# A fused attention and MLP kernel on one core: x^T in two PSUM tensors, four products ahead of the numerators, key features behind the numerators, last results by halves

## The chip, the core and the metric

The kernel runs on one core of a Trainium2 chip. A core has five engines with instruction streams of their own: PE (matrix products out of SBUF into PSUM), DVE and ACT (elementwise work; both read PSUM), POOL (elementwise work on SBUF) and SP (which here only starts DMA transfers). They meet through semaphores. The metric is the device time of one execution in microseconds; several executions are given as a median.

## The reference

Four batches of four heads, 1088 tokens, head dimension 32. Queries and keys are turned into 64 features each, and attention is linear in them; the result then goes through an MLP with an exact GELU.

```python
def phi(x):
    a = np.einsum('rd,bhsd->bhsr', S1, x)          # 8 values
    b = np.einsum('rd,bhsd->bhsr', S2, x)          # 8 values
    return np.einsum('bhsi,bhsj->bhsij', a, b).reshape(*x.shape[:-1], 64)
q_p, k_p = phi(q), phi(k)
kv  = np.einsum('bhsf,bhsd->bhfd', k_p, v)
z   = np.sum(k_p, axis=2)
num = np.einsum('bhsf,bhfd->bhsd', q_p, kv)
den = np.einsum('bhsf,bhf->bhs', q_p, z)[..., None] + 1e-06
x   = (num / den)                                   # then (B,H,S,D) -> (B*S, H*D) = (4352, 128)
h   = x @ w_in                                      # 128 -> 2048
g   = 0.5 * h * (1.0 + erf(h / sqrt(2)))
out = g @ w_out                                     # 2048 -> 128
```

## The kernel before

**Tiling.** Tokens are worked on in nine chunks. Chunks 0 to 7 have 512 tokens each, two for each batch; chunk 8 holds the 64 tokens left over from each of the four batches, 256 in all. For a chunk the kernel makes the query features (`expand_products`, `expand_copy`, `expand_multiply`), divides numerators by denominators (`attend_by_token` for chunks 0 and 1, `attend` for the others) into the transposed attention result x^T, and runs the MLP: 16 hidden products (`hidden`, L551), each 128 hidden channels wide, with a GELU on ACT (L558), and the products with w_out. Chunks 0 and 1 use plain projections (`project`, L667); chunks 2 to 7 replace these by Strassen-like products of half size (`two_products`, L624), whose sums of activations POOL forms (L593 to L596) and whose results `drain` and `combine` put together.

**Weights.** They arrive as 64-bit numbers. `Rounding` turns them into float32 in steps: `fields` (two DVE operations, L252 and L254, into `bits_e` and `bits_a`), `exponents` (ACT, L260, `bits_r`), `low_words` (ACT, L248, `bits_low`), `mantissas` (L268 on DVE, or L265 on ACT and L266 on POOL, `bits_m`), `signs` (DVE, L273, into `bits_e`), `product` (L278). The first two pieces of w_in and of w_out hold 256 columns, four hidden tiles in all: the first w_out piece serves the projections of tiles 0 and 1, the second those of tiles 2 and 3. Later pieces hold 512 columns.

**Keys.** For each batch `key_turn_blocks` turns the keys (DVE), `key_features` makes the two sets of eight values by 64 small PE products (L348, two calls of 32), copies one factor out with ACT (`a_t`, L361) and multiplies the outer product on DVE (`k_p`, L362). `add_tokens` adds token pairs, `kv_sum` forms kv on PE (L391), and `turn_kv` (L429) transposes it, through ACT copies `kv_T` and `kz`. `attend(n)` takes the numerators and denominators with four PE products (L494), copies the denominators out with ACT (`den`, L500, four copies), inverts them on DVE (L502), and multiplies (L506) into x^T.

**PSUM.** Eight banks: `h_ps` has two tensors of one bank (hidden products), `o_ps` two of one bank (projections), `w_ps` two of two banks (everything of attention). A reading engine is made to wait for another engine that reads the same PSUM tensor.

**Order.** It is written out by hand. A header runs the attention of batch 0 in straight lines. Behind it the steps are (chunk, hidden tile): chunks 0 and 1 alternate in groups of four tiles, then come chunks 2 to 8 of 16 tiles each. `at(t, f)` puts attention work into step t, `products`, `done` and `drains` do so for the other parts. In a step come the hidden product, then the slots, then stores, then products that fall due, two steps or more behind their GELU. The last lines of the function make every engine follow the order of the text.

The lines of the header and of the first steps that matter here:

```python
    attend_by_token(0, banks)
    ...
    w_in[1].product(pool)
    w_out[0].fields()
    turn_x(0, hidden_bank())
    ...
        if t == 3:
            attend_by_token(1, halves(work_banks()), lambda: (w_out[1].mantissas(), ...))
        if t == 4:
            turn_x(1, work_bank())
            for f, *a in products[t]:
                f(*a)
```

`turn_x` transposes the attention result of chunks 0 and 1 with four PE transposes into one PSUM tensor (L304); ACT copies its first half (L533), DVE its second (L534).

`store(8)`, at the end, copies the last chunk's two halves out of one PSUM tensor, the first with DVE and the second with ACT (L673), and starts two DMAs on SP and two on ACT's queue (L675).

Of the kernel before, what the change touches and what calls it, by code (L numbers as in the profile page):

```python
# [8 lines left out]
FP = mybir.dt.float32  # L9
# [7 lines left out]
def kernel(  # L17
# [20 lines left out]
    R = S1.shape[0]  # L38
# [196 lines left out]
    class Rounding:  # L235


        def __init__(self, dst):
            self.dst, self.wide = dst, dst.name in raw
            if self.wide:  # L240
                rows, n = dst.shape
                self.lo, self.hi = raw[dst.name][:, :, 0], raw[dst.name][:, :, 1]
                self.a, self.e, self.r = (mlp.tile([128, LC], U32, name=f"bits_{x}")[:rows, :n] for x in "aer")
                self.low, self.m = (mlp.tile([128, LC], FP, name=f"bits_{x}")[:rows, :n] for x in ("low", "m"))
# [55 lines left out]
    def transposed(ps, name, srcs, copy):  # L300

        n = len(srcs) * 128
        for i, s in enumerate(srcs):
            pe.transpose(ps[:, i * 128:(i + 1) * 128], in_=s, identity=ident)  # L304
        t = att.tile([128, CW], FP, name=name, bufs=3 if name == "xT" else 2)
        copy(out=t[:, :n], in_=ps[:, :n])
        return t
# [33 lines left out]

    def key_features(b, r, banks, by_pool=()):

        for i in range(2 * NCH):
            for c in range(2):
                for t in range(2):
                    at = i * 128 + c * 64
                    pe.matmul(banks[t][c * 64:(c + 1) * 64, i * 32:(i + 1) * 32],  # L348
                              lhsT=kT[r][t * 64:(t + 1) * 64, at:at + 64],
                              rhs=S12[t * 64:(t + 1) * 64, 2 * t:2 * t + 2].rearrange("p h r -> p (h r)"),  # L350
                              start=True, stop=True)

        k_p[b, r] = att.tile([128, 2, J, R, R], FP, name="k_p")
# [74 lines left out]
    def turn_kv(b, ps, copy):  # L428
        pe.transpose(ps[:, :128], in_=kv_T[b], identity=ident)  # L429
        copy(out=kz[b].rearrange("p c n -> p (c n)"), in_=ps[:, :128])  # L430
# [55 lines left out]
    def attend(n, meanwhile=lambda: None):  # L486

        W = width[n]
        owners = [(0, W, n // NCH)] if n < NMAIN else [(i * REM, (i + 1) * REM, i % 2 * 2 + i // 2) for i in range(B)]
        banks = halves(work_banks())  # L490
        for (c0, c1, b) in owners:
            for c in range(NP):
                for r in range(2):
                    pe.matmul(banks[r][c * F:(c + 1) * F, c0:c1], lhsT=kz[b][r * F:(r + 1) * F, c, :],  # L494
                              rhs=qp[n][r * F:(r + 1) * F, c, c0:c1], start=True, stop=True)
        den = att.tile([128, CW], FP, name="den")
        for h in range(H):
            c, r = h // 2, h % 2
            at = c * F + (1 - r) * D
            act.activation(out=den[h * D:(h + 1) * D, :W], in_=banks[r][at:at + D, :W], func=ACT.Copy, bias=1e-6)  # L500
        meanwhile()
        dve.reciprocal(out=den[:, :W], in_=den[:, :W])  # L502
# [27 lines left out]

    def turn_x(n, ps):
        def by_both(out, in_):
            by_act(out=out[:, :CW // 2], in_=in_[:, :CW // 2])  # L533
            by_dve(out=out[:, CW // 2:], in_=in_[:, CW // 2:])  # L534

        xT[n] = transposed(ps, "xT", [x_tok[n][:, j].rearrange("p h d -> p (h d)") for j in range(JC)], by_both)

# [47 lines left out]
    def token_sums(n, b):  # L585
# [4 lines left out]
        for j, (name, dtype) in enumerate((("bits_a", U32), ("bits_e", U32), ("bits_low", FP), ("bits_m", FP))):  # L590
            t = mlp.tile([128, LC], dtype, name=name)
            s[j + 1] = (t if dtype == FP else t.bitcast(FP)).rearrange("p (e x) -> p e x", e=2)
# [62 lines left out]

    def project(n, fi):
        first, final = fi == 0, fi == NF - 1
        if first:
            o_of[n] = out_bank() if n < NMAIN else work_bank()
        g = g_of.pop((n, fi))  # L660
        if n == NMAIN:

            for i in range(B // 2):
                pe.matmul(o_of[n][:, i * 128:(i + 1) * 128], lhsT=g[:, i * 128:(i + 1) * 128], rhs=w_tile(w_out_sb, fi),  # L664
                          start=(first and i == 0), stop=final, skip_group_check=True)
            return
        pe.matmul(o_of[n], lhsT=w_tile(w_out_sb, fi), rhs=g, start=first, stop=final)  # L667

    def store(n):
        oT = mlp.tile([128, JC, d_model], FP, name="oT")  # L670
        if n == NMAIN:
            for i, (copy, eng) in enumerate(((by_dve, sp), (by_act, act))):
                copy(out=oT[:, i, :], in_=o_of[n][:, i * 128:(i + 1) * 128])  # L673
                for b in (i, i + 2):
                    eng.dma_start(out=out[b * S + MAIN:(b + 1) * S, :], in_=oT[b // 2 * REM:(b // 2 + 1) * REM, i, :])  # L675
            return
# [75 lines left out]
    w_out = [Rounding(w) for w in w_out_sb[:2]]  # L752
    w_out[0].low_words()
# [4 lines left out]
    w_in[1].product(pool)  # L758
    w_out[0].fields()
    turn_x(0, hidden_bank())  # L760
    keep_busy(1, bank)
    w_out[0].exponents()
    expand_copy(1, 2)
    expand_multiply(1, 0)
    w_out[0].finish()
    w_out[1].low_words()

# [9 lines left out]
    def features(b, r):  # L777
        key_features(b, r, halves(work_banks()))

    held = {}  # L780
# [18 lines left out]

    at(0, expand_copy, 1, 3)  # L800
    at(0, expand_multiply, 1, 1)
    at(1, lambda: (w_out[1].fields(), w_out[1].exponents()))
    for i, (t0, t1) in enumerate(((4, 6), (8, 10), (12, 20))):
# [18 lines left out]
    for n in range(3, NCHUNK):  # L822
# [20 lines left out]
    for t, (n, fi) in enumerate(steps):  # L843
# [4 lines left out]
        elif n == NMAIN:  # L848
            at_ = max(t + LAG, (n * NF + 5) if fi < 3 else (n * NF + 6) if fi < 5 else 0)
            products[at_].append((project, n, fi))  # L850
            if fi == NF - 1:
                done[at_ + 1].append(n)
        elif fi % NB == NB - 1:
# [73 lines left out]
```

## Time and profile before

| what | value |
|---|---|
| three runs, median | 278.21 us (277.94 to 278.29) |
| the profiled execution | 278.03 us |
| its span in the profile | 276.2 us |
| PE instructions | 2209 |
| PE's granted clock over the span | 0.998 |
| DMA | 13.49 MB, 49 GB/s in the mean |

| stretch of the span, us | what runs | PE busy | DVE | ACT | POOL |
|---|---|---|---|---|---|
| 0 to 18.29 | loads, attention of batch 0 up to chunk 0's first hidden product | 15.93 | 14.39 | 11.84 | 7.12 |
| 18.29 to 26.63 | up to chunk 1's first hidden product | 8.28 | 6.88 | 4.25 | 1.28 |
| 26.63 to 66.00 | chunks 0 and 1, attention of batch 1 | 39.37 | 24.60 | 22.02 | 12.16 |
| 66.00 to 260.00 | chunks 1 to 7 | 194.00 | 100.65 | 99.48 | 124.22 |
| 260.00 to 272.10 | chunk 8 | 12.05 | 4.26 | 5.06 | 0.00 |
| 272.10 to 276.20 | last copies and stores | 0.00 | 0.28 | 0.27 | 0.00 |

A row of the profile's timeline gives the start in us, the duration, the engine, the line of the source, the operation, what it writes and reads, and shapes; in brackets the engine's idle time before it and who ended that. PEld is PE's weight load. A float32 product shows as two records, a float32 transpose as one, and small products that run side by side in parts of the array overlap; the tile shape of the array (128\*128, 128\*64, 64\*64, 32\*128) stands after the operands. Ends of PE records are modelled, so starts are the better measure.

### The profile page before, as it was taken

What the parts mean: (1) busy time and instruction counts of PE and PEld (TensorE: products, weight loads), DVE (VectorE), ACT (ScalarE), POOL (GpSimd) and SP (SyncE); (2) the same over time, 40 slices, a digit from 0 to 9 for tenths busy, and PEclk for the clock granted to TensorE, in tenths of its full rate; (3) what the DMA queues carried; (4) which work ended last, traced back from release to release, by engine and by line L of the source; (5) the groups of instructions that cost most, each with busy time, mean ns of one, the idle gap of its engine ahead of it and who ended that gap; (6) DMA issues with size and microseconds to landing.
All of it is one profiled execution on the core that took longest, in us unless ns stands there. A gap on an engine that the chain in (4) does not pass through costs nothing.

```text
span 276.2 us, 5543 instructions
## 1 busy us (share of the span) xinstructions
PE 269.6 (98%) x2209; PEld 134.9 (49%) x2209; DVE 151.1 (55%) x248; ACT 142.9 (52%) x282; POOL 144.8 (52%) x158
## 2 busy tenths in 40 slices
PE   8989999999999999999999999999999999999993
PEld 6744444543432455445444555444444454455793
DVE  6987688424953565079308965479037902750230
ACT  4683764356454634484348433674358344733441
POOL 3331000952003896457875877368766886777300
PEclk9999999999999999999999999999999999999999
DMA  6659263636201200000200001000200020011020
GB/s 210 188 155 325 47 167 62 160 76 161 42 0 29 34 16 2 2 0 1 40 0 1 2 2 34 7 0 2 38 0 2 0 40 0 1 24 18 4 38 19
DMA packets 37914, 13.49 MB, mean 49 GB/s; under 512 B 28288, under 2 KB 37248, under 8 KB 37888
## 3 DMA queue, kind: packets, MB, share of 16 engines
q1 hardware_dynamic: 37648, 13.05, 18.8%
q8 instruction: 17, 0.28, 0.5%
q10 hardware_dynamic: 240, 0.08, 0.1%
q14 instruction: 9, 0.07, 0.1%
HBM read 10.90 MB, written 2.23 MB: 48 GB/s over the span
## 4 chain that ended last, share of the span: by engine, by line
PE 96%; DVE 2%; ACT 0%; issue 0%
PE h_ps L551 43%; PE o_ps L624 27%; PE o_ps L667 10%; PE w_ps L453 3%; PE w_ps L664 3%; PE w_ps L494 2%; PE w_ps L391 1%; PE w_ps L696 1%; PE w_ps L348 1%; PE o_ps L400 1%; PE h_ps L304 1%; PE h_ps L520 0%; PE w_ps L420 0%; PE w_ps L520 0%; PE o_ps L304 0%
## 5 line engine op out<-in xcount | busy, mean ns | idle before, releaser
L551 PE MATMUL h_ps<-xT,w_in 128*64 128x512 f32 (+3 forms) x490 | 141.0, 577 | 1.1 <-DVE xT L534 1.0
L558 ACT ACTIVATE block<-h_ps 128x512 f32<-128x512 f32 (+1 forms) x112 | 63.4, 566 | 84.6 <-PE h_ps L551 83.7
L551 PEld LDWEIGHTS h_ps<-xT,w_in 128*64 128x64 f32 (+1 forms) x490 | 43.2, 146 | 38.0 <-issue 14.4
L593 POOL TENSOR_TENSOR bits_low<-block 128x512 f32<-128x512 f32 x24 | 30.8, 1284 | 52.8 <-ACT block L558 52.6
L624 PE MATMUL o_ps<-block,w_out 128*64 128x256 f32 x192 | 49.5, 380 | 0.0
L474 DVE TENSOR_TENSOR q_pT<-A_sb,w_ps 64x512 f32<-64x512 f32 x32 | 22.1, 691 | 43.0 <-ACT A_sb L460 42.3
L624 PEld LDWEIGHTS o_ps<-block,w_out 128*64 128x64 f32 x192 | 25.7, 137 | 32.4 <-issue 24.5
L594 POOL TENSOR_TENSOR bits_a<-block 128x512 f32<-128x512 f32 x24 | 30.6, 1274 | 12.9 <-ACT block L558 12.8
L667 PE MATMUL o_ps<-g,w_out 128*128 128x512 f32 x64 | 33.5, 604 | 0.0
L596 POOL TENSOR_TENSOR bits_m<-block,bits_e 128x512 f32<-128x512 f32 x24 | 30.6, 1276 | 1.9
L595 POOL TENSOR_TENSOR bits_e<-bits_a,block 128x512 f32<-128x512 f32 x24 | 30.6, 1274 | 1.9
L558 ACT ACTIVATE g<-h_ps 128x512 f32<-128x512 f32 x32 | 19.1, 596 | 21.2 <-PE h_ps L551 21.1
L502 DVE RECIPROCAL den<-den 128x512 f32<-128x512 f32 (+1 forms) x7 | 21.8, 3115 | 10.7 <-ACT den L500 10.7
L624 PE MATMUL o_ps<-bits_a,small 128*64 128x256 f32 x96 | 24.9, 382 | 0.0
L624 PE MATMUL o_ps<-bits_low,small 128*64 128x256 f32 x96 | 24.7, 380 | 0.0
L624 PE MATMUL o_ps<-block,small 128*64 128x256 f32 x96 | 24.7, 380 | 0.0
L624 PE MATMUL o_ps<-bits_m,w_out 128*64 128x256 f32 x96 | 24.6, 379 | 0.0
L624 PEld LDWEIGHTS o_ps<-block,small 128*64 128x64 f32 x96 | 13.0, 137 | 15.8 <-issue 11.7
L460 ACT COPY A_sb<-w_ps 64x512 f32<-64x512 f32 (+1 forms) x36 | 17.7, 557 | 3.1 <-PE w_ps L453 2.9
L506 DVE TENSOR_TENSOR xT<-w_ps,den 32x512 f32<-32x512 f32 (+1 forms) x28 | 18.2, 649 | 1.0
L667 PEld LDWEIGHTS o_ps<-g,w_out 128*128 128x128 f32 x64 | 11.3, 190 | 14.5 <-issue 13.6
L500 ACT ACTIVATE den<-w_ps 32x512 f32<-32x512 f32 (+1 forms) x28 | 15.6, 557 | 2.0 <-PE w_ps L494 1.7
(158 smaller groups left out, 295.9 us busy)
## 6 DMA issues: line engine op xcount, KB each, us to landing
block<-in_moe_w_in_dram SPq DMA_DIRECT2D x3, 512.0 KB, 7.9
block<-in_moe_w_out_dram SPq DMA_DIRECT2D x3, 512.0 KB, 10.6
k<-in_k_dram SPq DMA_DIRECT2D x48, 32.0 KB, 1.8
v<-in_v_dram SPq DMA_DIRECT2D x3, 512.0 KB, 4.3
q<-in_q_dram SPq DMA_DIRECT2D x24, 64.0 KB, 3.8
out_dram<-oT SPq DMA_DIRECT2D x24, 64.0 KB, 2.2
k<-in_k_dram SPq DMA_DIRECT2D x2, 256.0 KB, 3.1
q<-in_q_dram SPq DMA_DIRECT2D x2, 256.0 KB, 4.2
```

The costliest lines, as they stand in the source:

```text
L460: act.copy(out=A[g // 2][F:, g % 2, :width[n]], in_=B_of[n][g // 2][:F, g % 2, :width[n]])
L474: dve.tensor_mul(out=cols[r * F:(r + 1) * F], in0=a[:, :, r::2], in1=b[:, :, r::2])
L502: dve.reciprocal(out=den[:, :W], in_=den[:, :W])
L506: dve.tensor_mul(out=xT[n][rows, :W], in0=banks[h % 2][rows, :W], in1=den[rows, :W])
L551: pe.matmul(ps[rows, :W], lhsT=w[:, rows], rhs=xT[n][:, :W], start=True, stop=True)
L558: act.activation(out=g_of[n, fi][:, :W], in_=ps[:, :W], func=ACT.Gelu)
L593: pool.tensor_sub(out=s[3], in0=a11, in1=a21)
L594: pool.tensor_add(out=s[1], in0=a21, in1=a22)
L595: pool.tensor_sub(out=s[2], in0=s[1], in1=a11)
L596: pool.tensor_sub(out=s[4], in0=a12, in1=s[2])
L624: pe.matmul(acc[n][bank][half * 64:(half + 1) * 64, col:col + HW], lhsT=fixed, rhs=moving, start=b == 0 and e == 0 and name in "4715", sto ...
L667: pe.matmul(o_of[n], lhsT=w_tile(w_out_sb, fi), rhs=g, start=first, stop=final)
```

## The change

- **x^T of chunks 0 and 1.** `turn_x` takes two PSUM tensors, two transposes into each; ACT copies the first, DVE the second. `fields` of w_out's first piece moves ahead of the token attention of chunk 0.
- **Chunk 0's four hidden products first.** Steps 0 to 3 run only `hidden(0, t)`; then come chunk 1's numerators (`attend_by_token(1)`), then the projections of tiles 0 and 1, then chunk 1's transposes, the projection of tile 2 and chunk 1's first hidden product. The query features of chunk 1 are finished before step 0. The first w_out piece is finished on DVE in step 0; the second piece's mantissas move to ACT and POOL, its product from POOL to DVE.
- **Key features of batches 2 and 3.** They move from eleven steps behind the start of the chunk to five, into `attend`, right after the numerators; the 64 products share one PSUM tensor, the four `a_t` copies stand ahead of the `den` copies, and `k_p` and the token sums follow x^T. The key turns move from inside `attend` to seven steps ahead of it. Batch 1 stays as it was.
- **kv of batches 2 and 3** is turned by two 64-column float32 products with the identity in place of one transpose.
- **The last chunk** has a PSUM tensor for each half; the last two tiles' projections run half by half; three of the four last stores are on SP, one on ACT.
- `bits_a` and `bits_e` have three buffers each, `kT_rem` one of 128 columns.

```diff
-    def turn_x(n, ps):
-        def by_both(out, in_):
-            by_act(out=out[:, :CW // 2], in_=in_[:, :CW // 2])
-            by_dve(out=out[:, CW // 2:], in_=in_[:, CW // 2:])
-
-        xT[n] = transposed(ps, "xT", [x_tok[n][:, j].rearrange("p h d -> p (h d)") for j in range(JC)], by_both)
+    def turn_x(n, banks):
+
+        xT[n] = att.tile([128, CW], FP, name="xT", bufs=3)
+        for i, ps in enumerate(banks):
+            for j in range(2):
+                pe.transpose(ps[:, j * 128:(j + 1) * 128], in_=x_tok[n][:, 2 * i + j].rearrange("p h d -> p (h d)"),
+                             identity=ident)
+        for i, (ps, copy) in enumerate(zip(banks, (by_act, by_dve))):
+            copy(out=xT[n][:, i * 256:(i + 1) * 256], in_=ps[:, :256])
...
     def turn_kv(b, ps, copy):
-        pe.transpose(ps[:, :128], in_=kv_T[b], identity=ident)
+        if b < 2:
+            pe.transpose(ps[:, :128], in_=kv_T[b], identity=ident)
+        else:
+            for rows in (slice(0, 64), slice(64, 128)):
+                pe.matmul(ps[rows, :128], lhsT=kv_T[b][:, rows], rhs=ident, start=True, stop=True)
...
+        meanwhile()
         den = att.tile([128, CW], FP, name="den")
         for h in range(H):
...
-        meanwhile()
         dve.reciprocal(out=den[:, :W], in_=den[:, :W])
...
+    w_out = [Rounding(w) for w in w_out_sb[:2]]
+    w_out[0].fields()
     attend_by_token(0, banks)
...
-    turn_x(0, hidden_bank())
+    turn_x(0, [hidden_bank(), hidden_bank()])
...
+    def features_of_all(b):
+        banks = halves(work_banks())
+        for r in range(2):
+            key_products(r, banks, r * 128)
+        held["keys"] = banks
+        held["factors"] = []
+        for r in range(2):
+            a = att.tile([128, 2, J, 2 * R], FP, name="a_t")
+            for t in range(2):
+                act.copy(out=a[:, t, :, 0:R], in_=factors(banks[t], r)[:, :, 0:R])
+            held["factors"].append(a)
...
+    def outer_of_all(b):
+        for r, a in enumerate(held["factors"]):
+            k_p[b, r] = att.tile([128, 2, J, R, R], FP, name="k_p")
+            for t in range(2):
+                dve.tensor_mul(**spread(k_p[b, r][:, t], a[:, t, :, 0:R], factors(held["keys"][t], r)[:, :, R:2 * R]))
+        for r in range(2):
+            add_tokens(b, r, dve)
...
-        at(t + 5, attend, n, lambda b=b, keys=keys: [key_turn_blocks(b, r) for r in range(2) if keys])
         if keys:
+            for r in range(2):
+                at(t - 2, key_turn_blocks, b, r)
+        at(t + 5, attend, n, lambda b=b, keys=keys: keys and features_of_all(b))
+        if keys:
+            at(t + 5, outer_of_all, b)
             at(t + 8, widen_v_rem, b)
-            for r in range(2):
-                at(t + 11, features, b, r)
-            for r in range(2):
-                at(t + 11, add_tokens, b, r, dve)
...
+            if fi < NF - 2:
+                products[at_].append((project, n, fi))
             if fi == NF - 1:
+                products[at_] += [(project, n, f, (i,)) for i in range(B // 2) for f in (fi - 1, fi)]
                 done[at_ + 1].append(n)
...
     for t in range(len(steps) + LAG):
-        if t == 3:
-            attend_by_token(1, halves(work_banks()), lambda: (w_out[1].mantissas(), w_out[1].signs(),
-                                                              w_out[1].product(pool)))
+        if t < 4:
+            hidden(0, t)
+            if t == 0:
+                w_out[0].exponents()
+                w_out[0].finish()
+                w_out[1].fields()
+            if t == 3:
+                attend_by_token(1, halves(work_banks()), lambda: (w_out[1].exponents(), w_out[1].low_words(),
+                                                                  w_out[1].mantissas(by_pool=True)))
+                w_out[1].signs()
+                w_out[1].product()
+                for u in range(4):
+                    for f, *a in products[u]:
+                        f(*a)
+            continue
         if t == 4:
-            turn_x(1, work_bank())
+            turn_x(1, [work_bank(), work_bank()])
```

More of the change, by code (lines that the diff above doesn't have):

```diff
@@ L242, in __init__ @@
                 self.lo, self.hi = raw[dst.name][:, :, 0], raw[dst.name][:, :, 1]
-                self.a, self.e, self.r = (mlp.tile([128, LC], U32, name=f"bits_{x}")[:rows, :n] for x in "aer")
+                self.a, self.e, self.r = (mlp.tile([128, LC], U32, name=f"bits_{x}", bufs=2 if x == "r" else 3)[:rows, :n]
+                                          for x in "aer")
                 self.low, self.m = (mlp.tile([128, LC], FP, name=f"bits_{x}")[:rows, :n] for x in ("low", "m"))
@@ L304, in transposed @@
             pe.transpose(ps[:, i * 128:(i + 1) * 128], in_=s, identity=ident)
-        t = att.tile([128, CW], FP, name=name, bufs=3 if name == "xT" else 2)
-        copy(out=t[:, :n], in_=ps[:, :n])
+        t = att.tile([128, n], FP, name=name, bufs=1 if name == "kT_rem" else 2)
+        copy(out=t, in_=ps[:, :n])
         return t
@@ L340, in spread, with key_products @@
                     in1=b[:, :, None, :].broadcast_to([128, n, R, R]))
-    def key_features(b, r, banks, by_pool=()):
+    def key_products(r, banks, col=0):
         for i in range(2 * NCH):
@@ L347, in key_features @@
                     at = i * 128 + c * 64
-                    pe.matmul(banks[t][c * 64:(c + 1) * 64, i * 32:(i + 1) * 32],
+                    pe.matmul(banks[t][c * 64:(c + 1) * 64, col + i * 32:col + (i + 1) * 32],
                               lhsT=kT[r][t * 64:(t + 1) * 64, at:at + 64],
@@ L351, in key_features @@
                               start=True, stop=True)
+    def key_features(b, r, banks, by_pool=()):
+        key_products(r, banks)
         k_p[b, r] = att.tile([128, 2, J, R, R], FP, name="k_p")
@@ L590, in token_sums @@
         for j, (name, dtype) in enumerate((("bits_a", U32), ("bits_e", U32), ("bits_low", FP), ("bits_m", FP))):
-            t = mlp.tile([128, LC], dtype, name=name)
+            t = mlp.tile([128, LC], dtype, name=name, bufs=3 if dtype == U32 else 2)
             s[j + 1] = (t if dtype == FP else t.bitcast(FP)).rearrange("p (e x) -> p e x", e=2)
@@ L654, in combine, with project @@
         return N[:, 1]
-    def project(n, fi):
+    def project(n, fi, parts=range(B // 2)):
         first, final = fi == 0, fi == NF - 1
         if first:
-            o_of[n] = out_bank() if n < NMAIN else work_bank()
-        g = g_of.pop((n, fi))
+            o_of[n] = out_bank() if n < NMAIN else [work_bank() for i in range(B // 2)]
+        g = g_of[n, fi]
         if n == NMAIN:
-            for i in range(B // 2):
-                pe.matmul(o_of[n][:, i * 128:(i + 1) * 128], lhsT=g[:, i * 128:(i + 1) * 128], rhs=w_tile(w_out_sb, fi),
-                          start=(first and i == 0), stop=final, skip_group_check=True)
+            for i in parts:
+                pe.matmul(o_of[n][i][:, :128], lhsT=g[:, i * 128:(i + 1) * 128], rhs=w_tile(w_out_sb, fi),
+                          start=first, stop=final)
             return
@@ L672, in store @@
             for i, (copy, eng) in enumerate(((by_dve, sp), (by_act, act))):
-                copy(out=oT[:, i, :], in_=o_of[n][:, i * 128:(i + 1) * 128])
-                for b in (i, i + 2):
-                    eng.dma_start(out=out[b * S + MAIN:(b + 1) * S, :], in_=oT[b // 2 * REM:(b // 2 + 1) * REM, i, :])
+                copy(out=oT[:, i, :], in_=o_of[n][i][:, :128])
+                for b, queue in ((i, eng), (i + 2, sp)):
+                    queue.dma_start(out=out[b * S + MAIN:(b + 1) * S, :],
+                                    in_=oT[b // 2 * REM:(b // 2 + 1) * REM, i, :])
             return
@@ L751 @@
     keep_busy(1, bank)
-    w_out = [Rounding(w) for w in w_out_sb[:2]]
     w_out[0].low_words()
@@ L758 @@
     w_in[1].product(pool)
-    w_out[0].fields()
-    turn_x(0, hidden_bank())
+    turn_x(0, [hidden_bank(), hidden_bank()])
     keep_busy(1, bank)
[L762 to L766, printed above, removed]
+    for i in range(2):
+        for g in range(2):
+            if i:
+                expand_copy(1, 2 + g)
+        expand_multiply(1, i)
     steps = [(n, fi) for f in range(0, NF, 4) for n in range(2) for fi in range(f, f + 4)]
@@ L778, in features, with factors @@
         key_features(b, r, halves(work_banks()))
+    def features_of_all(b):
[9 more added lines that the diff above has]
+            held["factors"].append(a)
+    def factors(bank, r):
+        return bank[:, r * 128:(r + 1) * 128].rearrange("p (n r) -> p n r", r=2 * R)
+    def outer_of_all(b):
[5 more added lines that the diff above has]
+            add_tokens(b, r, dve)
     held = {}
@@ L798, in round_at @@
         at(t + 1, lambda: (r[0].exponents(), r[0].finish()))
-    at(0, expand_copy, 1, 3)
-    at(0, expand_multiply, 1, 1)
-    at(1, lambda: (w_out[1].fields(), w_out[1].exponents()))
     for i, (t0, t1) in enumerate(((4, 6), (8, 10), (12, 20))):
@@ L849 @@
             at_ = max(t + LAG, (n * NF + 5) if fi < 3 else (n * NF + 6) if fi < 5 else 0)
-            products[at_].append((project, n, fi))
+            if fi < NF - 2:
+                products[at_].append((project, n, fi))
             if fi == NF - 1:
+                products[at_] += [(project, n, f, (i,)) for i in range(B // 2) for f in (fi - 1, fi)]
                 done[at_ + 1].append(n)
```

## The prediction

> **What bounds the kernel now.** I read the page's busy shares and chain first, then the timeline of the places that the change touches.
>
> ```profile
> PE 269.6 (98%) x2209; PEld 134.9 (49%) x2209; DVE 151.1 (55%) x248; ACT 142.9 (52%) x282; POOL 144.8 (52%) x158
> ...
> PE 96%; DVE 2%; ACT 0%; issue 0%
> ```
>
> PE is busy 98% of the span and holds 96% of the chain, at full clock in all slices. So a microsecond counts only if PE itself spends or waits it; outside PE, only the opening and the tail are on the chain. The opening, by the timeline (start, us, engine, line):
>
> ```profile
> 16.93 0.72 POOL L278 TENSOR_TENSOR w_in<-bits_m,bits_e 128x256 f32<-128x256 f32 x1 [0.69 <-DVE bits_e L273]
> 16.98 0.83 DVE L254 TENSOR_SCALAR bits_a<-small 128x256 uint32<-128x256 uint32 x1
> 17.00 0.37 ACT L533 COPY xT<-h_ps 128x256 f32<-128x256 f32 x1
> ...
> 17.73 0.41 DVE L534 COPY xT<-h_ps 128x256 f32<-128x256 f32 x1
> ...
> 18.29 2.97 PE L551 MATMUL h_ps<-xT,w_in 128*128 128x512 f32 x6 [1.03 <-DVE xT L534]
> ...
> 25.75 0.37 ACT L533 COPY xT<-w_ps 128x256 f32<-128x256 f32 x1 [0.87 <-PE w_ps L304]
> 26.15 0.42 DVE L534 COPY xT<-w_ps 128x256 f32<-128x256 f32 x1 [1.15 <-ACT xT L533]
> ...
> 26.63 1.98 PE L551 MATMUL h_ps<-xT,w_in 128*128 128x512 f32 x4
> ```
>
> PE waits for DVE's half of x^T each time. At 26.15 that half starts only when ACT's half is read, though no data ties them: they read one PSUM tensor. At 17.73 it also stands behind bits_a, which takes 0.83 here and 0.28 elsewhere. From 26.63 on PE alternates hidden products and projections, 0.86 us each, without a gap that matters.
>
> **Opening, first half.** The fields of the first output weights move from after the token attention (16.78) to before it. There DVE is free: at 13.91 it does the fields of w_in, and its next work waits 0.54 for PE at 14.73. Two fields of 0.28 end at about 14.7, so they are hidden if that weight has landed: issued on SP by 7.8, and the small output weights land in at most 4.6, so 12.4. That cover gone, every microsecond of lateness goes into the attention. DVE's half of x^T then follows bits_e (ends 16.85) and runs beside ACT's: 17.0 to 17.4. Chunk 0 starts at about 17.5, not 18.29: 0.8 earlier.
>
> **Opening, second half.** All four hidden products of chunk 0 now stand ahead of chunk 1's numerators. With 0.86 us a product, 1.13 from start to its gelu (18.29 to 19.42), 0.60 a gelu and two PSUM banks, the third product waits for the first gelu, the fourth for the second. ACT: x^T to 17.4, two copies for the query features (1.06) to 18.45, gelu 0 to 19.25, bits_r (0.51), gelu 1 to 20.2, gelu 3 to 22.05. PE: products at 17.5, 18.4, 19.4, 20.3, ending at 21.2. DVE: four query multiplications (2.8) to 20.2, the first output weights (0.43 three times) to 21.5, fields to 22.0. Numerators (1.07) end at 22.3; two projections with the change of tile shape (1.05 + 0.86) at 24.15; four transposes (0.6) at 24.75. The tokens' DVE work (1.32) ends at 23.8, in time.
>
> What is late next is the second output weights, since projection 2 stands ahead of chunk 1's first product. After gelu 3 at 22.05, ACT does bits_r, bits_low, bits_high (0.51 + 0.44 + 0.42) to 23.45; POOL adds (0.72) to 24.2; DVE has bits_e (0.42), then the product (0.43). Here a rule and the rows decide. The 0.83 row is a DVE operation beside POOL's; likewise the additions of L383, 0.69 alone, took 1.13 at 104.38, beside POOL. The Trainium skill ("SBUF — State Buffer", section "SBUF: two separate sides") says why: VectorE and GpSimd share one pair of ports as an exclusive lock, also against a VectorE operation with two SBUF inputs. It speaks against this change: bits_e has two such inputs and becomes ready at 23.8, inside POOL's addition. Without the lock it ends at 24.2, the weights at 24.65 and chunk 1 starts after PE's own 24.75 plus 0.86, at 25.7. With it, bits_e ends at 24.6, the product at 25.0, and projection 2 runs 25.15 to 26.0. I take the lock, since the rows show it: chunk 1 starts at 26.0 against 26.63, **0.63 gained** (0.3 to 0.95). x^T of chunk 1 (both halves done by 25.45) hides under projection 2.
>
> **Key features.** Twice (batches 2 and 3) 64 small matmuls move from between hidden products to directly behind the numerators, which have the same 64*64 tile shape.
>
> ```profile
> 89.13 1.09 PE L494 MATMUL w_ps<-q_pT,kz 64*64 64x512 f32 x8
> 90.15 1.08 PE L551 MATMUL h_ps<-xT,w_in 128*64 128x512 f32 x4
> ...
> 99.24 1.03 PE L551 MATMUL h_ps<-xT,w_in 128*64 128x512 f32 x4
> 100.20 1.14 PE L348 MATMUL w_ps<-S,kT 64*64 64x32 f32 x64
> 101.26 0.65 PE L624 MATMUL o_ps<-bits_e,small 128*64 128x256 f32 x4
> 101.75 1.03 PE L551 MATMUL h_ps<-xT,w_in 128*64 128x512 f32 x4
> ```
>
> From hidden product to hidden product here is 2.51; one with four such records between would be 0.86 + 0.43 = 1.29. So the features cost 1.22, of which their weight loads fill 1.02; the rest is entering and leaving the shape, which the numerators pay already. Gain 0.19 each, **0.38 for both** (0.2 to 0.6). Their inputs come from DVE transposes (1.42) moved seven steps ahead: for batch 2 between the query multiplications and the outputs' turns, so chunk 0's turn moves from 82.64 to 84.1, while chunk 1's waits for PE until 85.59 anyway; for batch 3 into 11.49 in which DVE waits.
>
> The price is on ACT. The four a_t copies (pairs took 0.33) now precede the four den copies:
>
> ```profile
> 90.28 2.38 ACT L500 ACTIVATE den<-w_ps 32x512 f32<-32x512 f32 x4 [0.44 <-PE w_ps L494]
> 92.69 1.33 ACT L558 ACTIVATE block<-h_ps 128x512 f32<-128x512 f32 x2
> ```
>
> den waits for the features and a_t: about 1.0 + 0.66. It then ends at 94.3, the first gelu behind it at 94.95. The hidden product that needs its bank started at 94.07 and, shifted by 1.02, would start at 95.1, its weight load 0.2 earlier. Slack is nil: I take 0.08 of stall each, **0.15 lost** (0 to 0.8, the upper end if copies run one by one). DVE's chain behind (den 3.35, x^T 2.79, k_p 2.8, sums 2.7) ends at about 106 against a use at 109.2; POOL's sums start 1.6 later, with over 1 us left to their use.
>
> **kv turns of batches 2 and 3.**
>
> ```profile
> 111.56 1.03 PE L551 MATMUL h_ps<-xT,w_in 128*64 128x512 f32 x4
> 112.52 0.33 PE L429 MATMUL w_ps<-ident,kv_T 128*128 128x128 f32 x1
> ...
> 113.69 1.03 PE L551 MATMUL h_ps<-xT,w_in 128*64 128x512 f32 x4
> ```
>
> 2.13 between hidden products, elsewhere 1.72: the transpose costs 0.41. Against the change speaks "TensorEngine Tiling (Array Packing)", section "Restrictions": column tiling disables transpose mode for FP32, so the halves are ordinary FP32 matmuls. By the records of transposes (0.14 each in a row) doing it in one is cheaper, 0.14 against two pairs of half-width records; by the row of four 128*64 records of 256 columns (0.43), 128 columns take 0.22, or 0.30 if weight loads of 0.14 set the pace. The row counts the change of shape and decides: 0.15 each, **0.30 gained** (0.2 to 0.4; an extra load wait could make it nil).
>
> **Tail.** The chain's end:
>
> ```profile
> 270.71 1.35 PE w_ps L664 x12
> ...
> 272.09 0.30 DVE oT L673
> ...
> 272.42 0.27 ACT oT L673
> ```
>
> Then ACT issues two stores from 272.71, the second at 273.3, landing 1.9 later. Now the halves have PSUM tensors of their own and half 0 finishes first: four records (0.44) earlier. DVE copies at 271.65, ACT at 272.09 beside it. SP issues three stores of about 0.57: 271.97, 272.55, 273.1. The last starts at 273.1 instead of 273.3: **0.2 gained** (0.05 to 0.4; more if ACT's issue was the slow one).
>
> **Sum.** 0.63 + 0.38 - 0.15 + 0.30 + 0.20 = 1.36. The profiled execution took 278.03: span 276.2 and 1.83 outside, which nothing here touches. 278.03 - 1.36 = 276.67; it stands 0.18 below the median 278.21, within its spread. I predict **276.7**; other edits (buffers, names) cost nothing on PE, at most their waits.
>
> **Rivals.**
> - *No lock and no stall*: chunk 1 starts at 25.7 (0.93), nothing is lost on ACT: 0.93 + 0.38 + 0.30 + 0.20 = 1.81, 276.2. For it: PE's own work allows it. Against: the 1.13 row.
> - *Little arrives*: the second weights eat the opening (0.1 left) and ACT's burst the features: 0.1 + 0.38 - 0.8 + 0.30 + 0.20 = 0.18, 277.85. For it: nil slack behind den. Against: pairs of copies took 0.33.
> - *Slower*: the chain of the second output weights, 3 us long and now in front of chunk 1, comes late, one for one. At 1.36 us later than my 25.0 all gains are gone, and from there it decides; at 27.0 it gives 276.67 + 2.0 = 278.7. For it: seven steps on three engines behind gelu 3. Against: each step has its row, and before the weights were made by 24.5.
> - *The halves are still read in turn*: x^T 0 then ends at 17.8, 0.34 before now, and everything behind it shifts by 0.44, so chunk 1 starts at 26.44 (0.19 gained); the tail gains nothing: 0.19 + 0.38 - 0.15 + 0.30 = 0.72, 277.3. Against: DVE's copy now waits for PE alone.
>
> **How the numbers follow.** Forecast 60%, the high rival 14%, turn-taking 8%, little arrives 11%, slower 4%, others 3%. Below 0.2% (0.55 us) this kernel's measurement tells nothing from no change. Faster 0.89, same 0.07, slower 0.04. Range 276.0 to 277.6: the parts' bounds and the near rivals.
>
> **What would show it.** Hidden product 0 at 17.5 and chunk 1's first at 26.0; DVE's x^T copy beside ACT's; L494 and features in one block, with 3.0 between the hidden products around it (1.98 now, plus 1.02); no PE gap at the third hidden product after it; kv turns at 1.94 to 2.02 between hidden products; the two oT copies overlapping. Wrong: chunk 1 after 26.6, PE waiting on ACT after both attentions, or the last store issued 1.2 us or more after PE's end, as now.

## The result and the profile after

Four executions of the changed kernel took 276.38 us in the median (276.25 to 276.44), four of the kernel before beside them 278.11 (277.94 to 278.29). The ratio is 0.9937, with a 95% interval of 0.992 to 0.9954: 1.73 us less. The profiled execution took 276.43, its span 274.7. Of the page after, the first row of busy times and the shares of the chain:

```profile
PE 268.2 (98%) x2215; PEld 135.5 (49%) x2215; DVE 157.7 (57%) x248; ACT 142.5 (52%) x283; POOL 146.9 (53%) x158
...
PE 96%; DMA 1%; DVE 1%; issue 0%; ACTq 0%; ACT 0%; DVEq 0%
```

PE still holds 96% of the chain. Its busy time fell by 1.4; that of DVE grew by 6.6 and that of POOL by 2.1, and the end does not show it. So the gain lies in stretches between PE's own starts. The opening, in the timeline after (start, us, engine, line; line numbers are now up to 12 higher: `hidden` is L563, `project` L679):

```profile
13.14 0.90 PE L529 MATMUL h_ps<-kz,q_pT 64*64 64x33 f32 x47
...
14.69 0.47 PE L529 MATMUL h_ps<-kz,q_pT 64*64 64x33 f32 x17 [0.65 <-issue]
...
17.33 0.42 DVE L548 COPY xT<-h_ps 128x256 f32<-128x256 f32 x1 [0.17 <-PE h_ps L545]
17.35 0.37 ACT L548 COPY xT<-h_ps 128x256 f32<-128x256 f32 x1
...
17.91 3.83 PE L563 MATMUL h_ps<-xT,w_in 128*128 128x512 f32 x8 [0.18 <-DVE xT L548]
...
23.43 0.76 DVE L537 TENSOR_TENSOR x_tok<-w_ps,den_tok 128x256 f32<-128x256 f32 x2
23.54 0.73 POOL L267 TENSOR_TENSOR bits_m<-bits_high,bits_low 128x256 f32<-128x256 f32 x1 [5.57 <-ACT bits_high L266]
24.10 0.44 DVE L274 SCALAR_TENSOR_TENSOR bits_e<-small,bits_r 128x256 uint32<-128x256 uint32 x1
...
24.65 0.42 DVE L279 TENSOR_TENSOR w_out<-bits_m,bits_e 128x256 f32<-128x256 f32 x1
...
25.19 0.30 PEld L679 LDWEIGHTS o_ps<-g,w_out 128*128 128x128 f32 x2 [0.27 <-issue]
...
26.15 1.88 PE L563 MATMUL h_ps<-xT,w_in 128*128 128x512 f32 x4
```

The two copies of x^T now run beside each other. Ahead of 14.69, though, PE pauses in the middle of 64 records that wait for nothing this view shows. With the refill behind it this costs 0.88: the product behind these records starts 1.95 after their start, where the execution before had 1.06. A repeat without the pause (below) has its first hidden product 0.85 nearer to that start.

Starts taken out of the timelines make a ledger that can be compared from kernel to kernel. **Start** is where the token numerators of chunk 0 begin; **pause** from there to the query-feature products behind them; **A** from the transposes of x^T of chunk 0 to its first hidden product; **B** from there to chunk 1's first hidden product; **C** from the numerators that precede batch 2's features to batch 2's kv products (batch 3 agrees within 0.02); **D** from hidden product to hidden product around a kv turn; **E** from the last hidden product to the span's end. The span's end is taken to two digits. The last column is the median time with its range, or the time of a single execution.

| kernel | start | pause | A | B | C | D | E | time |
|---|---|---|---|---|---|---|---|---|
| before | 13.55 | 1.06 | 2.07 | 8.34 | 20.03 | 2.13 | 6.12 | 278.11 (277.94 to 278.29) |
| before, once more | 14.13 | 1.07 | 2.07 | 8.35 | 20.03 | 2.13 | 6.13 | 278.63 |
| after | 13.14 | 1.95 | 1.21 | 8.24 | 19.72 | 1.94 | 6.13 | 276.38 (276.25 to 276.44) |
| after, once more | 13.67 | 1.07 | 1.25 | 8.24 | 19.72 | 1.94 | 6.16 | 275.78 (275.65 to 276.14) |
| after, a third time | 13.86 | 1.06 | 1.26 | 8.23 | 19.71 | 1.94 | 6.11 | 276.17 (275.62 to 276.31) |
| before + x^T halves | 13.30 | 1.95 | 1.89 | 8.13 | 20.03 | 2.13 | 6.11 | 278.19 |
| before + halves + early fields | 13.12 | 1.07 | 1.25 | 8.09 | 20.03 | 2.14 | 6.12 | 276.42 |
| after, x^T in one tensor | 12.93 | 1.07 | 1.75 | 8.25 | 19.72 | 1.94 | 6.12 | 275.92 |
| after, old order of the opening | 13.49 | 1.06 | 1.26 | 8.07 | 19.72 | 1.94 | 6.14 | 275.82 (275.67 to 276.56) |
| after, features where they were | 14.04 | 1.31 | 1.21 | 8.25 | 20.03 | 1.94 | 6.12 | 276.88 (276.24 to 277.43) |
| after, kv by one transpose | 14.11 | 1.07 | 1.25 | 8.24 | 19.72 | 2.13 | 6.14 | 277.0 (276.04 to 277.76) |
| after, two stores a queue | 13.32 | 1.06 | 1.25 | 8.24 | 19.72 | 1.94 | 5.89 | 275.95 (275.53 to 276.11) |
| the same, projections in turn | 14.23 | 1.06 | 1.26 | 8.24 | 19.72 | 1.94 | 5.87 | 275.86 (275.6 to 276.43) |
| old order + two stores a queue | 14.03 | 1.31 | 1.21 | 8.12 | 19.72 | 1.94 | 5.89 | 275.75 (275.47 to 276.36) |

The inner stretches repeat within about 0.02 where their code is the same; only A is 0.04 shorter where there is a pause. What scatters is the start (12.93 to 14.23, with and without the change), the pause, and E by 0.05. So a part worth 0.2 is read from its stretch, not from the medians. The expectations below took E from spans rounded to a tenth, and their values of it (6.1, 6.18 to 6.21, 5.85) are up to 0.05 off.

The ledger closes. From before to after: start -0.41, pause +0.89, A -0.86, B -0.10, two C -0.62, two D -0.38, E +0.01, and 0.11 less behind B (chunk 1's first hidden product to the numerators of C, 62.50 before and 62.39 after; the product that had waited for x^T used to take 1.82 to its projection and now takes 1.71). Together -1.58; the spans, 276.24 and 274.65, differ by 1.59. Start and pause are not the change's own. Without them, and with A from the undisturbed executions (2.07 to 1.25, -0.82), the change is worth 0.82 + 0.10 + 0.11 + 0.62 + 0.38 - 0.01 = **2.02**. Two executions without a pause agree: the spans of before and of the first repeat of after, 276.24 and 274.35, differ by 1.89, with a start that lies 0.12 later in the repeat, so by 2.01 behind the start.

### The profile page after: what moved, and what is told of

The parts are those of the page before. It is cut to its first block, busy times and chain, and to the rows that moved or that the text cites. A ratio compares the mean times of both kernels' runs of the same rounds, so it can differ in the third digit from the quotient of the medians.

```text
span 274.7 us, 5546 instructions
## 1 busy us (share of the span) xinstructions
PE 268.2 (98%) x2215; PEld 135.5 (49%) x2215; DVE 157.7 (57%) x248; ACT 142.5 (52%) x283; POOL 146.9 (53%) x158
## 2 busy tenths in 40 slices
DMA packets 37914, 13.49 MB, mean 49 GB/s; under 512 B 28288, under 2 KB 37248, under 8 KB 37888
## 4 chain that ended last, share of the span: by engine, by line
PE 96%; DMA 1%; DVE 1%; issue 0%; ACTq 0%; ACT 0%; DVEq 0%
PE h_ps L563 43%; PE o_ps L636 27%; PE o_ps L679 11%; PE w_ps L461 3%; PE w_ps L676 3%; PE w_ps L503 2%; PE w_ps L395 1%; PE w_ps L349 1%; DMA raw_SR<-in_S_dram 1%; PE o_ps L404 1%; PE h_ps L529 0%; PE w_ps L424 0%; PE w_ps L529 0%; PE o_ps L305 0%; PE o_ps L709 0%
## 5 line engine op out<-in xcount | busy, mean ns | idle before, releaser
L563 PE MATMUL h_ps<-xT,w_in 128*64 128x512 f32 (+3 forms) x490 | 140.6, 576 | 0.2 <-DVE xT L548 0.2
L563 PEld LDWEIGHTS h_ps<-xT,w_in 128*64 128x64 f32 (+1 forms) x490 | 43.3, 146 | 35.7 <-issue 15.5
L605 POOL TENSOR_TENSOR bits_low<-block 128x512 f32<-128x512 f32 x24 | 31.5, 1312 | 50.5 <-ACT block L570 50.4
L679 PE MATMUL o_ps<-g,w_out 128*128 128x512 f32 x64 | 33.5, 607 | 0.1
L607 POOL TENSOR_TENSOR bits_e<-bits_a,block 128x512 f32<-128x512 f32 x24 | 31.3, 1305 | 1.9
L679 PEld LDWEIGHTS o_ps<-g,w_out 128*128 128x128 f32 x64 | 11.2, 189 | 14.3 <-issue 14.1
```

The costliest lines, as they stand in the source:

```text
L563: pe.matmul(ps[rows, :W], lhsT=w[:, rows], rhs=xT[n][:, :W], start=True, stop=True)
L605: pool.tensor_sub(out=s[3], in0=a11, in1=a21)
L607: pool.tensor_sub(out=s[2], in0=s[1], in1=a11)
```

## The experiments

### The same kernels again

The unchanged "after" was run twice more, and "before" profiled once more.

> The changed kernel once more, for the runs beside it. If the kz copy at 12.82 us (13.23 in the kernel before) and the gap of 0.65 us within the numerators of chunk 0 are chance of one execution, they change here; if they belong to the change, both stand again. Time 276.4 by either.

> The changed kernel beside these two: stretches as in its first two traces (8.24, 6.2), about 276.0 us.

> The kernel before once more. Its stretches should stand as in its first trace (4.74 to chunk 0's first product, 8.34 to chunk 1's, 20.03 and 2.13 twice, 6.1 at the end), whatever its start does; a start of chunk 0's numerators away from 13.55 us, or a gap of PE among them, would be chance of the execution and not of the change.

The repeats of after took 275.78 and 276.17, with ratios to before beside them of 0.9908 (0.989 to 0.9926) and 0.9913 (0.9899 to 0.9928); before once more took 278.63, beside 278.77. In both repeats the 64 records run without a pause, and in the first of them chunk 0's hidden product stands 3.92 behind their start (13.67 to 17.59), where the first profile had 4.77 with the pause in it and before had 4.74. So the pause isn't made by the change, and it hid the gain of the first half of the opening in the first profile: a start there that agrees with the start before would have been read as "nothing gained". The two repeats stand 0.2 to 0.6 below the first median. A pause in all four executions of the first measurement would do that, and so would other starts; only the profiled one can be seen.

The kept traces show what the pause goes with. The queue q8, which the page calls "instruction", moves one packet of 16 KB shortly before the token numerators. In the four kernels with a pause this packet starts at 12.31 to 12.64, in the ten others at 10.91 to 11.91. In all four, PE resumes with its 48th record, 2.30 to 2.39 behind the packet's start; in the ten others this record stands 2.45 to 3.79 behind it. So PE seems to wait there for its next instructions. That is read from 14 traces; no run moved the packet.

The start follows PE's own pace. The eight transposes of the first keys begin at 3.92 (within 0.01) in every profile. Their records start 0.21 apart at first and 0.11 apart later. The faster pace comes at 4.3 in after, whose eight take 1.20, and only behind all eight in the profile with the latest start (14.23), where they take 1.92. From the first key features (6.03 and 7.11 in these two) to the token numerators it is 7.11 to 7.13 in thirteen profiles and 7.37 in one, so the rest of the scatter lies ahead of them. The page's row of the granted clock, full in all slices, does not show this.

### The opening, first half: PSUM tensors, early fields, or both

The kernel before got the two PSUM tensors for x^T alone (and the buffers that go with them), then the early fields as well; the changed kernel got its one tensor back. With before and after these make a table of two by two.

Before + halves:

```diff
-    turn_x(0, hidden_bank())
+    turn_x(0, [hidden_bank(), hidden_bank()])
...
-            turn_x(1, work_bank())
+            turn_x(1, [work_bank(), work_bank()])
```

Before + halves + early fields:

```diff
+    w_out[0].fields()
     attend_by_token(0, banks)
...
-    w_out[0].fields()
     turn_x(0, [hidden_bank(), hidden_bank()])
```

After, x^T in one tensor (and `turn_x` as it was before):

```diff
-    turn_x(0, [hidden_bank(), hidden_bank()])
+    turn_x(0, hidden_bank())
```

> Kernel before with x^T in two PSUM tensors alone (with the buffers). If DVE's copy of chunk 0 is held by bits_a and not by ACT, the stretch from the numerators to chunk 0's first product stays at 4.7 us (4.74 before, 3.92 after); if the shared tensor holds it, it falls by about 0.4. In chunk 1 both theories free DVE's half by 0.4, of which projection 2 leaves 0.2: 8.34 to about 8.1.

> The same with the fields of the first output weights ahead of the token attention too. Numerators to first product 3.92 us if these two edits make the whole first part, about 4.3 if the order of the four products has a share in it. First product to chunk 1's first stays near 8.1; if it does, the four products ahead (8.24) bring nothing of their own.

> Changed kernel with x^T in one PSUM tensor read in turn. Numerators to first product 3.92 + 0.41 = 4.3 us (DVE's copy behind ACT's); first product to chunk 1's first stays 8.24, since projection 2 covers the second copy.

| stretch A | fields late | fields early |
|---|---|---|
| one PSUM tensor | 2.07 | 1.75 |
| two | 1.89 | 1.25 |

By the table the tensors alone bring 0.18 and the fields alone 0.32, together 0.82. But the 0.18 is not the tensors' own, as a line of before and then the timeline of before + halves show:

```profile
15.97 0.55 DVE L268 SCALAR_TENSOR_TENSOR bits_m<-bits_a,bits_low 128x256 f32<-128x256 uint32 x1
```

```profile
16.57 0.41 DVE L269 SCALAR_TENSOR_TENSOR bits_m<-bits_a,bits_low 128x256 f32<-128x256 uint32 x1
...
17.40 0.73 POOL L279 TENSOR_TENSOR w_in<-bits_m,bits_e 128x256 f32<-128x256 f32 x1 [1.40 <-DVE bits_e L274]
17.44 0.84 DVE L255 TENSOR_SCALAR bits_a<-small 128x256 uint32<-128x256 uint32 x1
...
18.20 0.41 DVE L540 COPY xT<-h_ps 128x256 f32<-128x256 f32 x1
```

DVE's copy no longer has to wait for ACT's (17.51, for 0.37), but it stands behind `bits_a`, which takes 0.84 beside POOL's product and 0.28 where it is issued early. It stood behind `bits_a` before, too. What got shorter is `bits_m`, three operations ahead of `bits_a`: it took 0.55 beside POOL's product (15.51 to 16.24), and 0.41 here, where the pause had moved it clear of that product (15.27 to 16.00). The transposes, where A begins, also come 0.03 later behind `x_tok`. That is 0.17 of the 0.18. From the numerators to the first hidden product this kernel took 5.45; without its pause (0.89) and with `bits_m` as before that is 4.70, against 4.74. So the tensors alone bring nothing that shows. In after with one tensor it is the other way round:

```profile
16.79 0.42 DVE L543 COPY xT<-h_ps 128x256 f32<-128x256 f32 x1 [0.54 <-ACT xT L542]
```

DVE is free and idles 0.54 until ACT has read the tensor. Two waits lay on one copy: that for `bits_a` ended last, and that for ACT's read some 0.3 before it. Taking away the earlier one alone brings nothing, taking away the later one 0.32, and both together 0.82. The time of the halves-only kernel, 278.19, is that of before (278.03 beside it), with a pause of 0.88 in its profile.

### The opening, second half: four products first

The changed kernel with the old order of the opening: the first steps run as before, with x^T halves and early fields kept.

```diff
-        if t < 4:
-            hidden(0, t)
...
-            if t == 3:
-                attend_by_token(1, halves(work_banks()), lambda: (w_out[1].exponents(), w_out[1].low_words(),
-                                                                  w_out[1].mantissas(by_pool=True)))
...
-            continue
+        if t == 3:
...
+            attend_by_token(1, halves(work_banks()), lambda: (w_out[1].mantissas(), w_out[1].signs(),
+                                                              w_out[1].product(pool)))
```

> Changed kernel with the opening's order of before (projections 0 and 1 between the hidden products), all else as changed. If the four products ahead cost PE 0.15 us, as 8.24 in the changed kernel against 8.09 in the kernel with x^T and fields alone says, first product to chunk 1's first takes 8.09 here and the rest is equal; the prediction's theory, that the order brings part of the opening's gain, asks for more than 8.24. The time, with half a microsecond of scatter at the start, should be 0.15 below the changed kernel's or not to be told from it.

B became 8.07 instead of 8.24 (before + halves 8.13, with early fields 8.09). So the order that gives this part its name does not bring B's gain over 8.34; either edit alone hides the turn-taking on chunk 1's x^T (new order with one tensor: 8.25), and of the two the tensors do it better. The timeline of the old order shows where the new one loses:

```profile
22.81 0.72 POOL L279 TENSOR_TENSOR w_out<-bits_m,bits_e 128x256 f32<-128x256 f32 x1 [5.19 <-DVE bits_e L274]
...
24.19 0.60 PE L545 MATMUL w_ps<-ident,x_tok 128*128 128x128 f32 x4
...
24.63 1.02 PE L679 MATMUL o_ps<-g,w_out 128*128 128x512 f32 x2
```

Here the second output weights are made by 23.53, one microsecond before use, and the projection follows the transposes by 0.44. In after it follows by 0.67 (24.55 to 25.22): the weights are done at 25.07 and PE's load of them starts at 25.19. The profile puts that idle 0.27 down to "issue", but in all the kernels with the new order the load starts 0.12 behind the end of this product (25.07 and 25.19, 24.74 and 24.86, 24.94 and 25.06), as it does behind DVE's x^T copy (17.75 and 17.87). Then the product behind it starts 0.93 later instead of 0.86. That is 0.30 lost against 0.14 saved by fewer changes of shape ahead of it (four products take 3.75, from 17.91 to 21.66, where three and one take 2.93 and 0.96).

### Key features

The features went back to eleven steps behind the start of the chunk, the key turns into `attend`.

```diff
-        meanwhile()
         den = att.tile([128, CW], FP, name="den")
...
+        meanwhile()
         dve.reciprocal(out=den[:, :W], in_=den[:, :W])
...
-        at(t + 5, attend, n, lambda b=b, keys=keys: keys and features_of_all(b))
+        at(t + 5, attend, n, lambda b=b, keys=keys: [key_turn_blocks(b, r) for r in range(2) if keys])
...
+                at(t + 11, features, b, r)
```

> Changed kernel with the key features of batches 2 and 3 back at eleven steps behind the chunk's start and the turns back inside attend. The prediction's sum gave the move 0.38 less 0.15 of stall: 0.23 slower than the changed kernel. The starts in the two traces (numerators to kv products 20.03 us before, 19.72 after, at both batches) say no stall and 0.31 each: 0.62 slower.

C returned to 20.03, in both batches, and all else stayed: 0.31 for a batch, 0.62 for both. The median, 276.88, lies 1.1 above that of after beside it; its profile has a later start (14.04) and a pause of 0.24 too. The block in PE's timeline of after, and then ACT's timeline behind it:

```profile
88.54 1.09 PE L503 MATMUL w_ps<-q_pT,kz 64*64 64x512 f32 x8
89.45 1.08 PE L349 MATMUL w_ps<-S,kT 64*64 64x32 f32 x64
90.47 1.08 PE L563 MATMUL h_ps<-xT,w_in 128*64 128x512 f32 x4
...
94.39 1.03 PE L563 MATMUL h_ps<-xT,w_in 128*64 128x512 f32 x4
```

```profile
90.60 0.56 ACT L804 COPY a_t<-w_ps 128x64 f32<-128x64 f32 x4 [1.35 <-PE w_ps L349]
91.17 2.39 ACT L510 ACTIVATE den<-w_ps 32x512 f32<-32x512 f32 x4
93.59 1.09 ACT L570 ACTIVATE block<-h_ps 128x512 f32<-128x512 f32 x2
```

From numerators to the next hidden product it was 1.02 and is 1.93, so the features add 0.91 here, where they added 1.22 between hidden products. They take 1.02 themselves; but they start 0.91 behind the numerators, behind which a product of another shape started 1.02 later. ACT does not hold PE: the first gelu behind `den` starts at 93.59, and the hidden products go on in their step of 1.72 (one at 92.67, the next at 94.39).

### kv turns

```diff
-        if b < 2:
+        if b < B:
             pe.transpose(ps[:, :128], in_=kv_T[b], identity=ident)
```

> Changed kernel with one transpose for kv of batches 2 and 3 again. The prediction gave 0.15 each, 0.30 slower; the two traces (2.13 us between hidden products before, 1.94 after) say 0.38 slower. [...]

D returned to 2.13 in both batches; nothing else moved. The median, 277.0, lies 1.2 above that of after beside it, with times from 276.04 to 277.76, more than the 0.38 of D. In the profiled executions the difference is accounted for: the spans, 275.17 and 274.35, differ by 0.82, of which 0.44 is a later start (14.11 and 13.67) and 0.38 is D. The chain of waits of after (start, us, what) gives the four records of a turn 0.22, between hidden products that have 1.72 from one to the next elsewhere:

```profile
111.69 0.22 PE w_ps L437 x4
```

### The tail

First the fourth store went back to ACT's queue, so that SP and ACT start two each; then the half-by-half order of the last projections was undone as well (the second diff).

```diff
-                for b, queue in ((i, eng), (i + 2, sp)):
+                for b, queue in ((i, eng), (i + 2, eng)):
```

```diff
-            if fi < NF - 2:
-                products[at_].append((project, n, fi))
+            products[at_].append((project, n, fi))
...
-                products[at_] += [(project, n, f, (i,)) for i in range(B // 2) for f in (fi - 1, fi)]
```

> Changed kernel with two last stores on SP and two on ACT. If the third store on SP (its issue starts at about 271.7 us) ate the gain of the halves, the last issue starts about 0.25 us earlier and the time falls by about 0.2; if the end is set by something else than the last issue, it stays.

> Changed kernel with two stores on each queue and the last projections tile by tile again. If the half-by-half order buys the end something, the end moves back by up to 0.4 us from last hidden product to end of span (5.85 with two stores each). If the last issue is ACT's second, whose half is the last in either order, the stretch stays at 5.85 or falls by the 0.07 that PE's last records lost in the half-by-half order.

E is 6.11 to 6.16 in after, 6.12 and 6.13 before, 5.89 with two stores a queue and 5.87 with the projections in turn as well. The end in the timeline of after, then with two stores a queue (SPq and ACTq are the queues' issues):

```profile
270.12 0.29 DVE L685 COPY oT<-w_ps 128x128 f32<-128x128 f32 x1 [6.57 <-PE w_ps L676]
270.44 1.87 SPq L687 DMA_DIRECT2D out_dram<-oT  x3
270.57 0.27 ACT L685 COPY oT<-w_ps 128x128 f32<-128x128 f32 x1 [1.02 <-PE w_ps L676]
270.86 0.54 ACTq L687 DMA_DIRECT2D out_dram<-oT  x1
```

```profile
269.77 1.17 SPq L687 DMA_DIRECT2D out_dram<-oT  x2
...
270.19 1.20 ACTq L687 DMA_DIRECT2D out_dram<-oT  x2
```

SP's three issues run from 270.44 to 272.31, while ACT is done at 271.40; the third starts at 271.71, which is 1.18 behind PE's end (270.53), where the last store before started 1.23 behind it. Two and two end at 270.94 and 271.39, or 1.53 behind PE's end at 269.86 and not 1.78. The half-by-half order lets DVE copy 0.15 earlier (1.60 behind the last hidden product, not 1.75) and costs PE 0.07 (its last twelve records take 1.57, not 1.50, so that ACT's copy comes at 2.05 and not 1.98): nothing comes of it at the end.

So the parts of the tail come apart. With two stores a queue and the projections in turn, only the two PSUM tensors are left of the change, and E is 0.25 shorter than before (6.12 to 5.87). The half-by-half order adds 0.02 to that, and the third store on one queue 0.24: together they use up what the tensors bring.

### What the runs point to

The old order of the opening with two stores a queue, and all the rest of the change:

> The same with two last stores on each queue: last hidden product to end of span 5.85 us in place of 6.18 to 6.21. With both edits the sum is 0.48 below the changed kernel: about 275.5 where the changed kernel has 276.0.

It took 275.75 (275.47 to 276.36), a ratio to before of 0.9908 (0.9892 to 0.9924); after beside it took 276.17 (275.62 to 276.31). B is 8.12 and E 5.89, so by the ledger it is some 0.1 and 0.2 ahead of after; its profile has a pause of 0.24. The times overlap and do not tell the two apart.

## Why the prediction was right, and where its steps were not

The time was right, 276.7 against 276.38, and so were the direction and the range. That it came so near is in part luck: the sum of 1.36 was not that of the parts, which is 2.02, and in the first profile a pause of 0.88 took from the difference while a start 0.41 earlier added to it. Of the repeats, 276.17 lies within the range and 275.78 below its lower end of 276.0.

| step | predicted | measured | shown by |
|---|---|---|---|
| opening, both halves | 0.63 | 0.82 + 0.10 + 0.11 = 1.03 | A, B, and the product behind B |
| key features | 0.38 | 0.62 | C, undone and done |
| ACT's stall behind them | -0.15 | 0 | no gap at 94.39 |
| kv turns | 0.30 | 0.38 | D, undone and done |
| tail | 0.20 | -0.01 (-0.04 to 0.02) | E |

- **Opening, first half.** Predicted 0.79 (18.29 to 17.5), measured 0.82. The prediction named both waits on DVE's copy and took both away; the experiments show that the fields alone bring 0.32, the tensors alone nothing, and the tensors 0.50 once the fields are early (1.75 to 1.25).
- **Opening, second half.** PE's own sum was right: the first projection was put 4.8 behind the first hidden product and stands 4.82 behind it (17.91 and 22.73). That the second output weights are late next was right too. What failed is the term for the **lock**: chunk 1 was to start 8.5 behind chunk 0, and starts 8.24 behind. The weights were to be done at 24.65 without the lock and at 25.0 with it, that is 7.15 or 7.5 behind the first hidden product; they are done 7.16 behind. The step before that was mis-sized: ACT's three operations behind gelu 3 take 1.02 from its end (22.37 to 23.39), since each starts before the one ahead has ended, and not 0.51 + 0.44 + 0.42. So POOL's addition ended at 24.27, when `bits_e` had only just come up behind `x_tok`. The rule of the shared ports isn't refuted: `bits_a` took 0.84 beside POOL in the halves-only kernel. It had little left to meet here: the records of `bits_e` and of POOL's addition overlap for 0.17 (24.10 to 24.27), and `bits_e` took 0.44, where its like at 21.00, with POOL idle, took 0.42. Held by a full lock until 24.27 it would have ended at about 24.7, and it ended at 24.54; POOL's recorded ends are rough, so this decides nothing about the lock. The rival "no lock and no stall", at 14%, describes the mechanism better than the forecast did, and by its sum of 1.81 is nearer to the parts.
- **Key features.** The mechanism was right and the size short. 0.19 counted one change of shape that goes; the runs show 0.31. The missing 0.11 is at the joint, 0.91 from numerators to features where 1.02 was carried over.
- **ACT.** "a_t 0.66" was 0.56 and overlapped; the stall of 0.08 for each batch did not appear.
- **kv turns.** The row of 0.22 was right; 0.30 as the pace of weight loads was too careful. The prediction's 0.14 for a transpose in a row of its like is the record of its weight load; the transposes themselves start 0.11 apart. The Trainium skill ("TensorEngine Tiling (Array Packing)", section "Restrictions") states that column tiling disables the transpose mode for FP32. No run here tries that, and the section sets no price on ordinary products. They cost 0.22 in the chain, and the one transpose with its change of shape 0.41. Had ordinary products been the dearer way, the kernel with one transpose would have been faster; its D is 0.19 longer at each turn.
- **Tail.** The overlap of the copies was right, the gain was not. By PE's end the first two of SP's stores stand where they were put (0.09 ahead of it, 0.49 behind it). The step that failed is the third: it was to start 1.03 behind PE's end and starts 1.18 behind, since 0.70 lie between the second issue and it, and not 0.55. That is just short of the prediction's own sign of being wrong, 1.2. And PE's half-by-half order moves its end by 0.07, which the sum left out.
- Of the other rivals, turn-taking is out by the copies at 17.33 and 17.35, "little arrives" by C, and "slower" by the weights at 25.07.

What stays open: why the instruction packet and PE's faster pace come earlier in one execution than in another. Both vary with and without the change, and no run was made for their cause. That the four executions of the first measurement all had the pause fits their times and isn't shown.

## What to carry to other kernels

Where one instruction stands under two waits, taking away the one that ends first shows nothing, though it is worth 0.50 here once the other is gone; list all that holds the instruction, and try the edits in a table of two by two. See what else differs between its cells: a pause in one of them passed for a gain of 0.18. When an engine is 98% busy, put work of the same tile shape together before looking at its waits: two edits of 64 and 4 small products brought half of this gain. And count issues on each queue at the end of a kernel: an overlap won in the copies was lost again to a third store on one queue.

## What the runs showed of the hardware

- PE can pause in the middle of 64 independent records. It was seen in 4 of 14 profiles, always ahead of the 48th of the token numerators of the opening: 0.88 twice and 0.24 twice, and in two of three executions of the same code not at all. The four are those in which a packet of 16 KB on the queue that the profile calls "instruction" starts at 12.31 or later; PE resumes 2.30 to 2.39 behind its start.
- PE starts at half its later pace (transposes 0.21 apart, then 0.11), and the change comes at 4.3 us in one profile and behind 5.4 in others. The start of the token numerators follows it, between 12.93 and 14.23 us, while stretches of 20 to 62 us behind it repeat within 0.03.
- Changing PE's tile shape has a price of its own: 64 products cost 1.22 between products of another shape and 0.91 behind some of the same shape, and a transpose that takes 0.11 from start to start in a row of its like costs 0.41 between products of shape 128\*64.
- On ACT, consecutive operations overlap in the records (in after): 0.50, 0.42 and 0.40 are the durations of three that end 1.02 behind the gelu ahead of them.
